# One copy for two pairs' attention output, and the first batch's tokens scaled with the batch they ride with

## The chip, the cores and the metric

The kernel runs on one core of one Trainium2 chip. The metric is device time in microseconds for one execution. The five engines are named as in the profile: PE (matrix multiply; PEld is its weight load), DVE (vector), ACT (scalar), POOL (GpSimd) and SP, which here only issues DMAs.

## The reference

With q and k of shape (8 batches, 12 heads, 448 tokens, 64) and v alike, the reference computes attention with a sigmoid in place of a softmax, joins the heads to 768 columns, and passes the result through a gated layer:

```python
scores = scale * np.matmul(q, k.transpose(0, 1, 3, 2)) - np.log(S)
attn = 1.0 / (1.0 + np.exp(-scores))
x = np.matmul(attn, v)                                   # heads joined: (8, 448, 768)
...
for k in range(K):                                       # K = 5
    gate_pre += conv_w[k][None, None, :] * xp[:, k:k + S, :]   # xp: x with 4 zero tokens ahead
gate = 1.0 / (1.0 + np.exp(-gate_pre))
val = x @ w_val
return (gate * val @ w_out)
```

All inputs and outputs are fp32.

## The kernel before, in words

**Work units.** A *pair* is two heads of one batch; there are 48 (six per batch), numbered i. Two pairs make a *two*, numbered j (24, three per batch). The columns of x that a pair yields are 128 of the 768, so a pair's x lies in SBUF as 128 partitions by 448 tokens.

**Attention.** For each pair, `scores` (L486 to L500) multiplies three blocks of 128 keys by the queries into a PSUM tile of two banks, one per head; the last 64 keys of both pairs of a two go through `scores_rest` (L502 to L513) into one such tile. `attention` (L515 to L532) applies the sigmoid on ACT. `attend` (L556 to L596) multiplies by the values: one PSUM tile `px` of two banks takes the x of both pairs of a two, bank p for pair p. It is written by five pieces of PE work that follow each other: the rest's (L578), then for p = 0 and p = 1 the key blocks 0 and 1, and the key block 2 (L586). All of these tiles come from one ring, `ps_a`, of three tiles, in the order rest, px, three for the even pair, three for the odd pair.

**Two precisions.** fp32 operands are multiplied in one of two ways. In the sets `WHOLE` (of twos, for attention times values) and `WHOLE_SCORES` (of pairs, for scores) the operands stay fp32. Otherwise they are split into a high and a low part and three cheaper products are summed: for `attend` in fp16, with values scaled by a power of two found by `v_scale` (L534 to L553) from the largest value (L564, spread over partitions by the matmul L574, read by DVE at L541); for scores by a copy and a subtraction (`split_qk`). A whole two needs one ACT operation for each score tile (L519) where a split one needs two on ACT (L519, L359) and one on DVE (L530).

**After attention.** `after` (L600 to L650) runs for each pair: it copies bank p of px to the tile x (L353 or L359 on ACT, L355 on DVE), finds the largest value on DVE (L619), and for batches 1 to 7 computes the gate: a copy of four tokens between segments (L641), the first tap (L359), four more taps on DVE (L647), a sigmoid (L650). Batch 0 has no products of its own: its 448 tokens are cut into seven runs of 64, and run f - 1 rides as 64 more columns with batch f, so that every product has 512 columns. So x of batch 0 goes to HBM (`first_x`) and a run of it is loaded with each later x tile (L634).

**Scaled products.** `x_scale` (L655) finds a batch's scale, `x_split` (L681) makes the high and low fp16 parts xs (L359 on ACT, L694 on DVE). In this version batch 0 has its own scale (`first_scale`), is split by itself, goes to HBM (`first_xs`) and comes back by run as the last 64 columns of xs. `product` (L702) multiplies 128 output columns: 18 matmuls of 512 columns (L716). For `val` DVE multiplies by the gate (L726), and the result g is split again; for `out` the result y is scaled in two operations, 448 columns with the batch's scale and 64 with batch 0's (L359 or L361), and stored by two DMAs.

**What sets the order.** Nothing is ordered by hand. Every operation is recorded with its possible engines, a cost, a priority (`tau` of its pair plus an entry of the table `AT`) and the buffers that it reads and writes; `Plan.issue` simulates the engines and so fixes the order in which each engine's instructions are emitted. The instructions then run in that order on each engine, and wait on semaphores that the tile layer derives from the tiles which each instruction touches. `Buf.part()` tells the plan that a part of a buffer may be used apart from the rest: in `attend`, `s["px"]` holds px and a part of it, so the plan takes the two banks as separate.

Of the kernel before, what the change touches and what calls it, by code (L numbers as in the profile page):

```python
# [10 lines left out]
F32 = mybir.dt.float32  # L11
# [13 lines left out]
KT = 5  # L25
P = 128
# [12 lines left out]
WHOLE = {*range(8)}  # L39
WHOLE_SCORES = {*range(15), 18}  # L40
# [33 lines left out]
    first=8.83, step=12.31, val=-38.5, val_step=7.32, out=-6, out_step=18.88, w_max=-5.5, w_split=-21.5,  # L74
    load_qk_first=-114, load_qk=93, load_v=-82, split_hi=38.5, split_lo=-9, rest_first=32, rest=138.5,
    a_first=-120, a=-70, attend=36, v_max=-106.5, v_exp=-11.5, v_split=-127, x=-60, x_max=-103,
    x_scale=-274, x_hi=-25, x_lo=-170, x_step=6.37, tap=81, scores=72, a_rest=38, a_rest_first=-111.5,
    tap_step=3.36, gate=-67.5, product=26, y=-45, g_hi=11, g_lo=-52.5, o=0.5, w_load=-41.5,
# [169 lines left out]
def attention_then_gate(  # L248
# [48 lines left out]
    x_ring = ring(sb, 9, [P, SEGS, HALO + SL], F32, "x")  # L297

    xs_ring = ring(sb, 8, [P, 2, T], F16, "xs")
# [31 lines left out]
    first_x = [scratch([P, HALO + S], F32, f"first_x{c}") for c in range(NC)]  # L331
    first_xs = [scratch([P, 2, S], F16, f"first_xs{c}") for c in range(NC)]
    first_scale = fixed([P, NC], F32, "first_scale")
# [153 lines left out]
    def scores(i, c):  # L487
# [11 lines left out]
        cost = (0.77 if i in WHOLE_SCORES else 0.61) + (0.1 if c == 0 else 0)  # L499
        return op({"P": cost}, tau(i) + AT["scores"], emit, sources(i), [b])  # L500

    def scores_rest(j):  # L502


        b = two[j]["ps"] = ps_a.new()
        x = [st[2 * j + n]["qk"] for n in range(2)]

        def emit(e):
            for n, to in enumerate(halves):
                for h, rows in enumerate(halves):  # L510
                    mm(b()[to, h, :S], x[n]()[rows, CW:], x[n]()[rows, :S], start=True, stop=True)  # L511

        return op({"P": 0.95}, tau(2 * j) + AT["rest_first" if 2 * j < AHEAD else "rest"], emit, x, [b])  # L513
# [20 lines left out]
    def v_scale(j):  # L534
# [3 lines left out]
        x, e, px = s["v"], v_exp.new(), two[j - 1]["px"][0]  # L538
        s["e"] = e
        col = lambda n: e()[:, n : n + 1]  # L540
        op({"V": 0.08}, tau(2 * j) + AT["v_exp"], lambda _: nc.vector.tensor_scalar(  # L541
            col(0), px()[:, 0, S : S + 1].bitcast(I32), 0x7F800000, None, op0=ALU.bitwise_and), [px], [e], port="")
# [13 lines left out]
    def attend(j):  # L556
# [3 lines left out]
        px, single, m = ps_a.new(), j in WHOLE, None  # L560
        s["px"] = px, px.part()
        if j + 1 < TWOS and j + 1 not in WHOLE:
            m, x = vm.new(), two[j + 1]["v"]
            op({"V": 0.98}, t + AT["v_max"], lambda e: nc.vector.tensor_reduce(  # L564
                m(), x(), axis=AX.X, op=ALU.max, apply_absolute_value=True), [x], [m], port="")
# [23 lines left out]
        last = first = op({"P": 0.87 if single else 0.75}, t, rest, [s["a"], *values] + ([ones, m] if m else []), s["px"])  # L589
        for p in range(2):  # L590
            for cs in ((0, 1), (2,)):
                last.then = op(
                    {"P": (0.82 if single else 0.64) * len(cs)}, t, lambda e, p=p, cs=cs: chunks(p, cs),
                    [*(st[2 * j + p]["a", c] for c in cs), *values], [s["px"][p]])
                last = last.then
# [4 lines left out]
    def after(i):  # L600

        s, t = st[i], tau(i - i % 2 + 2)
        p, f, c = i % 2, i // NP, i % NP
        px, whole = two[i // 2]["px"][p], i // 2 in WHOLE
        got = lambda: two[i // 2]["px"][0]()[:, p, :S]
        if c == 0:
            xm[f] = x_max.new()

        def out_of_ps(to, x):
            if whole:  # L610
                op({"A": 0.45, "V": 0.53}, t + AT["x"], lambda e: copy(e, to(), got()), [], [x, px], port="")
            else:
                v = two[i // 2]["e"]
                op({"A": 0.55}, t + AT["x"], lambda e: scaled(
                    e, to(), got(), v()[:, 3:4].bitcast(F32)), [v], [x, px], port="")

        def largest(to, x):
            b = xm[f]
# [3 lines left out]
        if f == 0:  # L622
            x = s["x"] = x_ring.new(lambda: sb.tile([P, HALO + S], F32, name="x_first", tag="x", bufs=x_ring.n))
            to = lambda: x()[:, HALO:].rearrange("p (s n) -> p s n", n=SL)
            s["own"], s["tokens"] = x, to
            op({"G": 0.1}, t - 8, lambda e: nc.gpsimd.memset(x()[:, :HALO], 0.0), [], [x], port="")
            out_of_ps(to, x)
            op({"S": 0.45}, t + 2, lambda e: nc.sync.dma_start(first_x[c](), x()), [x], [first_x[c]], P * 1800)
            largest(to, x)
            return  # L630
        x, g = s["x"], s["g"] = x_ring.new(), gate_ring.new()
        own, edge = x.part(), x.part()
        n = (f - 1) * SL
        op({"S": 0.45}, t - 8, lambda e: nc.sync.dma_start(  # L634
            x()[:, SEGS - 1, :], first_x[c]()[:, n : n + HALO + SL]), [first_x[c]], [x], P * 544)
        op({"G": 0.1}, t - 8, lambda e: nc.gpsimd.memset(x()[:, 0, :HALO], 0.0), [], [edge], port="")
        to = lambda: x()[:, : SEGS - 1, HALO:]
        s["own"], s["tokens"] = own, to
        out_of_ps(to, own)
        largest(to, own)  # L640
        op({"V": 0.1}, t + AT["tap"] - 0.5, lambda e: nc.vector.tensor_copy(  # L641
            x()[:, 1 : SEGS - 1, :HALO], x()[:, : SEGS - 2, SL:]), [own], [edge])
        by = lambda tile: tile.rearrange("p (s n) -> p s n", s=SEGS)
        w = lambda j: cw()[:, c, KT - 1 - j : KT - j]
        op({"A": 0.63, "V": 0.43}, t + AT["tap"], lambda e: scaled(e, by(g()), x()[:, :, HALO:], w(0)), [x, own, cw], [g])
        for j in range(1, KT):
            op({"V": 0.67}, t + AT["tap"] + AT["tap_step"] * j, lambda e, j=j: nc.vector.scalar_tensor_tensor(  # L647
                by(g()), x()[:, :, HALO - j : HALO + SL - j], w(j), by(g()), op0=ALU.mult, op1=ALU.add),
               [x, own, edge, cw], [g])
        op({"A": 0.55}, t + AT["gate"], lambda e: nc.scalar.activation(g(), g(), AF.Sigmoid), [], [g])  # L650
# [4 lines left out]
    def x_scale(b):  # L655
# [3 lines left out]
        for c in range(NP):  # L659
            st[b * NP + c]["xe"] = e  # L660
# [10 lines left out]
    def x_unscale(b):  # L671
        t = tau((b + 1) * NP) + AT["x_scale"] + 10
        e = st[b * NP]["xe"]
        to = outer[b] = o_scale.new() if b else first_scale
# [5 lines left out]
    def x_split(i):  # L680
        s, f, c = st[i], i // NP, i % NP  # L681
        t = tau((f + 1) * NP) + AT["x_step"] * c
        tokens, own, e = s["tokens"], s["own"], s["xe"]
        xs = s["xs"] = xs_ring.new()
        if f:
            n = (f - 1) * SL
            op({"S": 0.45}, t - 8, lambda _: nc.sync.dma_start(
                xs()[:, :, S:], first_xs[c]()[:, :, n : n + SL]), [first_xs[c]], [xs], P * 512)
        high, low = (xs.part() if f else xs), xs.part()
        s["xs_in"] = [xs, high, low]  # L690
        part = lambda n: xs()[:, n, :S].rearrange("p (s n) -> p s n", n=SL)
        sc = lambda: e()[:, 1:2].bitcast(F32)
        op({"A": 0.56, "V": 0.59}, t + AT["x_hi"], lambda eng: scaled(eng, part(0), tokens(), sc()), [own, e], [high])
        op({"V": 0.6}, t + AT["x_lo"], lambda _: nc.vector.scalar_tensor_tensor(  # L694
            part(1), tokens(), sc(), part(0), op0=ALU.mult, op1=ALU.subtract), [own, e, high], [low])
        if f == 0:
            op({"S": 0.45}, t + 2, lambda _: nc.sync.dma_start(first_xs[c](), xs()[:, :, :S]), [xs, low], [first_xs[c]], P * 1800)
# [4 lines left out]
    def product(n, b, m):  # L702
# [184 lines left out]
```

## Time and profile before

| | |
|---|---|
| three timed runs, median (lowest to highest) | 611.48 us (611.26 to 613.67) |
| the profiled execution | 611.03 us, of which the trace's span is 609.3 us |
| mean granted TensorE clock | 0.999 |
| PE busy | 580.9 us |
| DVE, ACT, POOL busy | 491.4, 409.3, 89.9 us |

The span runs from the first to the last instruction of the trace; the 1.7 us beside it lie around it. Of the views used, the windows give each engine's busy time in a stretch, the waits say for whom an engine sat idle, the timeline lists instructions with the idle time ahead of them, the groups sum instructions by line and shape, and the chain follows the work that ended last from releaser to releaser.

### The profile page before, as it was taken

The page shows a single profiled execution, that of the slowest core. Times are in us where ns is not written, and L with a number is a line of the kernel's source. Part 1 is how long each engine was busy: PE and PEld are TensorE (multiplying, and loading weights), DVE is VectorE, ACT ScalarE, POOL GpSimd, SP SyncE. Part 2 cuts the span into 40 slices and gives each one's busy share as a digit, 9 for nine tenths or more (in the row PEclk, how much of TensorE's full clock was granted, in tenths as well). Part 3 has the DMA queues.
Part 4 walks back from the last instruction along what each step waited for, and adds up shares of the span by engine and source line. Part 5 has one row for each costly group of instructions (what it writes and reads, how often), then busy time and mean ns, then how long its engine had stood idle before and what let it go on. Part 6 is the DMA issues. An engine that isn't in the chain of part 4 may idle for free.

```text
span 609.3 us, 9673 instructions
## 1 busy us (share of the span) xinstructions
PE 580.9 (95%) x3562; PEld 275.5 (45%) x3562; DVE 491.4 (81%) x893; ACT 409.3 (67%) x577; POOL 89.9 (15%) x120
## 2 busy tenths in 40 slices
PE   8899989999999999999999999999999999999996
PEld 4233324344444545444454444544444454444442
DVE  1899999899999889898888988879897797853310
ACT  5579877576985678857688676787757887642111
POOL 0000003210222212121221311113121131000000
PEclk9999999999999999999999999999999999999999
DMA  8998632232340332303234031341213300011011
GB/s 337 365 292 266 193 116 95 66 79 65 97 115 27 100 98 67 109 30 100 61 105 110 30 95 44 120 112 36 67 38 126 115 23 1 9 52 55 0 36 69
DMA packets 44351, 59.74 MB, mean 98 GB/s; under 512 B 25872, under 2 KB 33552, under 8 KB 44304
## 3 DMA queue, kind: packets, MB, share of 16 engines
q1 hardware_dynamic: 44304, 59.13, 31.0%
q8 instruction: 28, 0.46, 0.3%
q14 instruction: 19, 0.16, 0.1%
HBM read 45.34 MB, written 13.77 MB: 97 GB/s over the span
## 4 chain that ended last, share of the span: by engine, by line
PE 88%; DVE 5%; ACT 5%; issue 1%; ACTq 0%; DVEq 0%
PE ps_m L716 52%; PE ps_a L496 14%; PE ps_a L586 14%; PE ps_a L511 3%; PE ps_a L578 3%; ACT x L359 2%; ACT a_single L519 1%; DVE gate L647 1%; DVE x_max L619 1%; ACT y L359 1%; DVE w_words L381 1%; PE ps_m L751 1%; ACT xs L359 0%; ACT x L353 0%; DVE w_words L404 0%
## 5 line engine op out<-in xcount | busy, mean ns | idle before, releaser
L716 PE MATMUL ps_m<-g,w_out_hi 128*128 128x512 f16 x504 | 150.1, 379 | 1.4 <-DVE y L361 0.8
L716 PE MATMUL ps_m<-xs,w_val_hi 128*128 128x512 f16 x504 | 150.1, 379 | 0.8 <-DVE y L361 0.4
L364 POOL TENSOR_TENSOR qk_lo<-qk_src,qk_hi 128x448 fp32r<-128x448 f32 x64 | 81.8, 1291 | 305.2 <-DVE qk_hi L355 207.3
L647 DVE SCALAR_TENSOR_TENSOR gate<-x,cw,gate 128x512 f32<-128x512 f32 x168 | 125.5, 768 | 0.4 <-ACT gate L359 0.2
L519 ACT ACTIVATE ps_a<-ps_a 128x896 f32<-128x896 f32 x112 | 98.7, 902 | 17.5 <-PE ps_a L496 16.2
L530 DVE SCALAR_TENSOR_TENSOR a<-ps_a,a 128x896 f16<-128x896 f32 x96 | 101.4, 1084 | 9.2 <-ACT a L359 8.0
L716 PE MATMUL ps_m<-g,w_out_lo 128*128 128x512 f16 x252 | 95.5, 379 | 0.0
L716 PE MATMUL ps_m<-xs,w_val_lo 128*128 128x512 f16 x252 | 95.5, 379 | 0.0
L359 ACT ACTIVATE a<-ps_a 128x896 f16<-128x896 f32 x96 | 84.6, 920 | 0.4
L716 PEld LDWEIGHTS <-w_out_hi 128*128 128x128 f16 x504 | 48.0, 98 | 62.1 <-issue 5.9
L716 PEld LDWEIGHTS <-w_val_hi 128*128 128x128 f16 x504 | 47.8, 98 | 62.4 <-issue 7.5
L586 PE MATMUL ps_a<-a,v_hi 128*64 128x448 f16 x384 | 53.1, 355 | 11.6 <-ACT x L359 11.6
L519 ACT ACTIVATE a_single<-ps_a 128x896 f32<-128x896 f32 x56 | 47.3, 923 | 5.4 <-PE ps_a L496 3.6
L359 ACT ACTIVATE y<-ps_m,o_scale 128x448 f32<-128x448 f32 x35 | 21.5, 629 | 42.4 <-PE ps_m L716 35.3
L353 ACT CAST g<-y 128x512 f16<-128x512 f32 x24 | 14.8, 618 | 50.8 <-DVE y L726 50.5
L726 DVE SCALAR_TENSOR_TENSOR y<-ps_m,y_scale,gate 128x512 f32<-128x512 f32 x42 | 29.6, 742 | 20.3 <-PE ps_m L716 20.3
L586 PE MATMUL ps_a<-a_single,v_src 128*64 128x448 f32 x192 | 39.6, 547 | 6.2 <-ACT x L353 2.9
L650 ACT ACTIVATE gate<-gate 128x512 f32<-128x512 f32 x42 | 26.1, 626 | 26.5 <-DVE gate L647 26.3
L619 DVE TENSOR_REDUCE x_max<-x 128x1 f32<-128x448 f32 x42 | 25.8, 614 | 21.1 <-ACT x L359 19.0
L496 PE MATMUL ps_a<-qk_single 64*128 64x448 f32 x192 | 40.1, 554 | 0.4 <-ACT a_single L519 0.4
L359 ACT ACTIVATE x<-ps_a,v_exp 128x448 f32<-128x448 f32 x32 | 20.3, 634 | 29.5 <-PE ps_a L586 25.4
L496 PE MATMUL ps_a<-qk_hi 64*128 64x448 f32 x192 | 38.5, 397 | 0.0
(110 smaller groups left out, 728.0 us busy)
## 6 DMA issues: line engine op xcount, KB each, us to landing
qk_src<-qk SPq DMA_DIRECT2D x32, 448.0 KB, 4.0
v_src<-vs SPq DMA_DIRECT2D x24, 448.0 KB, 3.4
out_t<-y SPq DMA_DIRECT2D x42, 224.0 KB, 2.0
qk_single<-qk SPq DMA_DIRECT2D x16, 448.0 KB, 5.5
w_words<-w_val SPq DMA_DIRECT2D x6, 768.0 KB, 9.4
w_words<-w_out SPq DMA_DIRECT2D x6, 768.0 KB, 4.9
x<-first_x SPq DMA_DIRECT2D x42, 34.0 KB, 2.0
first_x<-x_first SPq DMA_DIRECT2D x6, 226.0 KB, 5.7
```

The lines of the kernel that those rows point to most:

```text
L359: nc.scalar.activation(to, x, AF.Copy, scale=by)
L364: engines[eng].tensor_tensor(to, x, y, op=ALU.subtract)
L496: mm(b()[:, h, :S], k()[rows, at : at + P], q()[rows, :S], start=(n == 0), stop=(n == len(terms(i)) - 1))
L511: mm(b()[to, h, :S], x[n]()[rows, CW:], x[n]()[rows, :S], start=True, stop=True)
L519: nc.scalar.activation(to, b()[:, :, :S], AF.Sigmoid, bias=-math.log(S), scale=1.0 / math.sqrt(D))
L530: op({"V": 1.0}, t + 0.5, lambda e: nc.vector.scalar_tensor_tensor(part(1), p(), A_SCALE, part(0), op0=ALU.mult, op1=ALU.subtract), [b], [ ...
L586: mm(px()[to, p, :S], v()[:, o : o + D], x(st[2 * j + p]["a", c])[:, h, at : at + S], start=False, stop=(c == 2 and n == len(parts) - 1), ...
L619: op({"V": 0.52}, t + AT["x_max"], lambda e: nc.vector.tensor_reduce(b()[:, c : c + 1], to(), axis=AX.XY, op=ALU.max, apply_absolute_value ...
L647: op({"V": 0.67}, t + AT["tap"] + AT["tap_step"] * j, lambda e, j=j: nc.vector.scalar_tensor_tensor(by(g()), x()[:, :, HALO - j : HALO + S ...
L650: op({"A": 0.55}, t + AT["gate"], lambda e: nc.scalar.activation(g(), g(), AF.Sigmoid), [], [g])
L716: mm(po(), w()[:, c, :], x()[:, k, :], start=(c == 0 and j == 0), stop=(c == NC - 1 and j == 2))
L726: op({"V": 0.6}, t + AT["y"], lambda e: nc.vector.scalar_tensor_tensor(y(), po(), y_scale()[:, m : m + 1], gate(), op0=ALU.mult, op1=ALU.m ...
```

## The change

1. `attend` writes px as one buffer, and `after` runs once for each two: one operation copies both banks (2 x 448 columns) into one tile x of two pairs, which has one load of batch 0's run, one search for the largest value and one edge copy. The ring of x has 5 such tiles (was 9 single ones), that of xs 4 (was 8).
2. Batch 0 has no scale, no split and no `first_xs`: the largest value of a batch f is taken over its own tokens and the run that rides with it, one `x_split` operation takes 2 x 512 columns, and y of an `out` product is scaled by one operation of 512 columns. Batch 0's tokens are thus rounded with another scale than before.
3. The search for the largest value of v and its matmul move from `attend`, where they used a column of px of the two before, to `scores_rest`, where they use a column of the rest's bank; DVE reads it there (`v_exp`).
4. `WHOLE` is now twos 0 to 8 and 21 (was 0 to 7), `WHOLE_SCORES` pairs 0 to 14, 17, 24, 39, 42, 43 (was 0 to 14 and 18).
5. The priorities in `AT` and some costs have other numbers; two lines of the table stand here for all.

```diff
-WHOLE = {*range(8)}
-WHOLE_SCORES = {*range(15), 18}
+WHOLE = {*range(9), 21}
+WHOLE_SCORES = {*range(15), 17, 24, 39, 42, 43}
...
-    first=8.83, step=12.31, val=-38.5, val_step=7.32, out=-6, out_step=18.88, w_max=-5.5, w_split=-21.5,
+    first=8.2, step=11.51, val=-64.5, val_step=38.05, out=-42, out_step=46.57, w_max=-113, w_split=-46.5,
...
-    x_ring = ring(sb, 9, [P, SEGS, HALO + SL], F32, "x")
-    xs_ring = ring(sb, 8, [P, 2, T], F16, "xs")
+    x_ring = ring(sb, 5, [P, 2, SEGS, HALO + SL], F32, "x")
+    xs_ring = ring(sb, 4, [P, 2, 2 * T], F16, "xs")
...
     def scores_rest(j):
+        if j not in WHOLE:
+            m, v = vm.new(), s["v"]
+            op({"V": 0.98}, t + AT["v_max"], lambda e: nc.vector.tensor_reduce(
+                m(), v(), axis=AX.X, op=ALU.max, apply_absolute_value=True), [v], [m], port="")
         def emit(e):
+            if m:
+                mm(b()[:, 0, S : S + 1], ones(), m(), start=True, stop=True)
...
+        if m:
+            e = s["e"] = v_exp.new()
+            op({"V": 0.08}, t + AT["v_exp"], lambda _: nc.vector.tensor_scalar(
+                e()[:, :1], b()[:, 0, S : S + 1].bitcast(I32), 0x7F800000, None, op0=ALU.bitwise_and), [], [b, e], port="")
...
     def attend(j):
-        s["px"] = px, px.part()
+        s["px"] = px
...
-    def after(i):
+    def after(j):
-        got = lambda: two[i // 2]["px"][0]()[:, p, :S]
-                op({"A": 0.45, "V": 0.53}, t + AT["x"], lambda e: copy(e, to(), got()), [], [x, px], port="")
+            got = lambda: px()[:, :, :S].rearrange("p t (s n) -> p t s n", n=SL)
+                op({"A": 0.82, "V": 1.0}, t + AT["x"], lambda e: copy(e, to(), got()), [], [x, px], port="")
-                op({"A": 0.55}, t + AT["x"], lambda e: scaled(
+                op({"A": 0.95}, t + AT["x"], lambda e: scaled(
                     e, to(), got(), v()[:, 3:4].bitcast(F32)), [v], [x, px], port="")
...
-            op({"V": 0.52}, t + AT["x_max"], lambda e: nc.vector.tensor_reduce(
-                b()[:, c : c + 1], to(), axis=AX.XY, op=ALU.max, apply_absolute_value=True), [x], [b], port="")
+        op({"V": 1.1}, t + AT["x_max"], lambda e: nc.vector.tensor_reduce(
+            b()[:, 2 * c : 2 * c + 2], x()[:, :, :, HALO:], axis=AX.XY, op=ALU.max, apply_absolute_value=True),
+           [x, own], [b], port="")
...
     def x_split
-            op({"S": 0.45}, t - 8, lambda _: nc.sync.dma_start(
-                xs()[:, :, S:], first_xs[c]()[:, :, n : n + SL]), [first_xs[c]], [xs], P * 512)
-        op({"A": 0.56, "V": 0.59}, t + AT["x_hi"], lambda eng: scaled(eng, part(0), tokens(), sc()), [own, e], [high])
+        op({"A": 1.16, "V": 1.19}, t + AT["x_hi"], lambda eng: scaled(eng, part(0), tokens(), sc()), [x, own, e], [high])
...
     def product
-            op({"A": 0.54, "V": 0.6}, t + AT["o"], lambda e: scaled(e, y()[:, :S], po()[:, :S], col(b)), [outer[b]], [y, po], port="")
-            op({"A": 0.21, "V": 0.2}, t + AT["o"], lambda e: scaled(e, y()[:, S:], po()[:, S:], col(0)), [po, outer[0]], [low], port="")
+            op({"A": 0.61, "V": 0.66}, t + AT["o"], lambda e: scaled(
+                e, y(), po(), outer[b]()[:, m : m + 1]), [po, outer[b]], [y], port="")
```

**What the new order looks like.** On ACT, from the sigmoid of the rest's tile of two 12 (`ps_a_2267`) on, while PE multiplies two 11 by its values into `ps_a_2279`, there stood before:

```order
L519 ACTIVATE ps_a_2267<-ps_a_2267 128x2x448
L650 ACTIVATE gate_2052<-gate_2052 128x512
L359 ACTIVATE a_rest_2315<-ps_a_2267 128x2x448
L650 ACTIVATE gate_2146<-gate_2146 128x512
L359 ACTIVATE x_1685<-ps_a_2279,v_exp_2061 128x7x64
L359 ACTIVATE gate_2338<-x_1685,cw_68 128x512
L359 ACTIVATE x_1693<-ps_a_2279,v_exp_2061 128x7x64
L359 ACTIVATE gate_2369<-x_1693,cw_68 128x512
L359 ACTIVATE v_hi_2380<-v_src_1858,v_exp_2347 128x896
L519 ACTIVATE ps_a_2352<-ps_a_2352 128x2x448
```

At the same two now (`ps_a_1936` is the rest's tile, `ps_a_1948` is px, the three tiles behind are the next pair's scores), ACT has:

```order
L531 ACTIVATE ps_a_1936<-ps_a_1936 128x2x448
L359 ACTIVATE a_rest_1982<-ps_a_1936 128x2x448
L648 ACTIVATE gate_1894<-gate_1894 128x512
L359 ACTIVATE x_1658<-ps_a_1948,v_exp_1694 128x2x7x64
L531 ACTIVATE ps_a_2013<-ps_a_2013 128x2x448
L531 ACTIVATE ps_a_2021<-ps_a_2021 128x2x448
L359 ACTIVATE a_2038<-ps_a_2013 128x2x448
```

The two copies of px with a tap between them have become one, which stands ahead of the sigmoids of the next scores; the first taps and the splitting of v have moved elsewhere.

On DVE around the same place there stood before, from the second half of the rest's tile on:

```order
L530 SCALAR_TENSOR_TENSOR a_rest_2315<-ps_a_2267,a_rest_2315 128x2x448
L619 TENSOR_REDUCE x_max_1784<-x_1685 128x1
L541 TENSOR_SCALAR v_exp_2347<-ps_a_2279 128x1
L641 COPY x_1685<-x_1685 128x6x4
L543 TENSOR_SCALAR v_exp_2347<-v_exp_2347 128x1
L647 SCALAR_TENSOR_TENSOR gate_2338<-x_1685,cw_68,gate_2338 128x512
L545 TENSOR_SCALAR v_exp_2347<-v_exp_2347 128x1
```

And now, where the first two rows are the gating of the products that PE finished just ahead of the rest:

```order
L717 SCALAR_TENSOR_TENSOR y_1942<-ps_m_1878,y_scale_103,gate_1044 128x512
L717 SCALAR_TENSOR_TENSOR y_1944<-ps_m_1884,y_scale_103,gate_1085 128x512
L523 TENSOR_SCALAR v_exp_1961<-ps_a_1936 128x1
L645 SCALAR_TENSOR_TENSOR gate_1894<-x_1176,cw_68,gate_1894 128x512
L552 TENSOR_SCALAR v_exp_1961<-v_exp_1961 128x1
L364 TENSOR_TENSOR g_1946<-y_1942,g_1946 128x512
L554 TENSOR_SCALAR v_exp_1961<-v_exp_1961 128x1
L364 TENSOR_TENSOR g2_1964<-y_1944,g2_1964 128x512
L556 TENSOR_SCALAR v_exp_1961<-v_exp_1961 128x1
L645 SCALAR_TENSOR_TENSOR gate_1894<-x_1176,cw_68,gate_1894 128x512
L542 SCALAR_TENSOR_TENSOR a_rest_1982<-ps_a_1936,a_rest_1982 128x2x448
L361 TENSOR_SCALAR v_hi_2017<-v_src_1509,v_exp_1961 128x896
```

The read of v's largest value (`v_exp`, first row of it) has moved from px to the rest's tile and from behind the rest's work to ahead of it.

On PE the pieces of a two stand in the same order as before, but the first pair of products stands behind the eighth attention times values (it stood behind the seventh), so that about 20 products are left behind the last one where 16 were.

More of the change, by code (lines that the diff above doesn't have):

```diff
@@ L559, in attend @@
         s, t = two[j], tau(2 * j + 2) + AT["attend"]
-        px, single, m = ps_a.new(), j in WHOLE, None
-        s["px"] = px, px.part()
[L562 to L565, printed above, removed]
+        px, single = ps_a.new(), j in WHOLE
+        s["px"] = px
         values = [s["v"]] if single else [s["vh"], s["vl"]]
@@ L587, in chunks @@
                            start=False, stop=(c == 2 and n == len(parts) - 1), skip_group_check=True)
[L589 removed]
+        last = first = op({"P": 0.86 if single else 0.8}, t, rest, [s["a"], *values], [px])
         for p in range(2):
             for cs in ((0, 1), (2,)):
[L592 to L594 removed]
+                cost = (0.752 if single else 0.567) * len(cs) + (0.13 if p and cs == (2,) else 0)
+                last.then = op({"P": cost}, t, lambda e, p=p, cs=cs: chunks(p, cs),
+                               [*(st[2 * j + p]["a", c] for c in cs), *values], [px])
                 last = last.then
@@ L622, in after @@
[L622 to L630, printed above, removed]
@@ L646, in after @@
[L646 to L650, printed above, removed]
+            x()[:, :, SEGS - 1, :], first_x[c]()[:, :, n : n + HALO + SL]), [first_x[c]], [x], P * 1088)
@@ new lines, in after @@
+        by = lambda tile: tile.rearrange("p (s n) -> p s n", s=SEGS)
+        for p in range(2):
+            g = st[2 * j + p]["g"] = gate_ring.new()
+            w = lambda k, p=p: cw()[:, 2 * c + p, KT - 1 - k : KT - k]
+            at = t + AT["tap"] + AT["tap_pair"] * p
+            op({"A": 0.63, "V": 0.43}, at, lambda e, p=p, g=g, w=w: scaled(
+                e, by(g()), x()[:, p, :, HALO:], w(0)), [x, own, cw], [g])
+            for k in range(1, KT):
+                op({"V": 0.67}, at + AT["tap_step"] * k, lambda e, p=p, g=g, w=w, k=k: nc.vector.scalar_tensor_tensor(
+                    by(g()), x()[:, p, :, HALO - k : HALO + SL - k], w(k), by(g()), op0=ALU.mult, op1=ALU.add),
+                   [x, own, edge, cw], [g])
+            op({"A": 0.55}, t + AT["gate"] + AT["tap_pair"] * p, lambda e, g=g: nc.scalar.activation(
+                g(), g(), AF.Sigmoid), [], [g])
@@ L658, in x_scale @@
         m, d, e, po = xm[b], diagonal.new(), x_exp.new(), ps_m.new()
-        for c in range(NP):
-            st[b * NP + c]["xe"] = e
+        for c in range(3):
+            two[3 * b + c]["xe"] = e
         col = lambda n: e()[:, n : n + 1]
@@ L672, in x_unscale @@
         t = tau((b + 1) * NP) + AT["x_scale"] + 10
-        e = st[b * NP]["xe"]
-        to = outer[b] = o_scale.new() if b else first_scale
+        e = two[3 * b]["xe"]
+        to = outer[b] = o_scale.new()
         op({"V": 0.06}, t, lambda _: nc.vector.tensor_scalar(
@@ L821, in attention_then_gate @@
             continue
+        x_scale(b)
+        for c in range(3):
+            x_split(3 * b + c)
         if b > 1:
```

117 lines of the change are left out of this document (49 added, 68 removed).

## The prediction

> **What bounds the kernel now.** I read the engines' totals, then stretches of 26 us, then PE's own waits, then one repeat of the loop in order of time. The totals (busy us, share of the span, instructions), the granted clock by slices, and the chain's shares by engine:
>
> ```profile
> PE 580.9 (95%) x3562; PEld 275.5 (45%) x3562; DVE 491.4 (81%) x893; ACT 409.3 (67%) x577; POOL 89.9 (15%) x120
> ...
> PEclk9999999999999999999999999999999999999999
> ...
> PE 88%; DVE 5%; ACT 5%; issue 1%; ACTq 0%; DVEq 0%
> ```
>
> PE is the bound nearly everywhere, at the full clock. The span of 609.3 us less 580.9 leaves 28.4 us of idle PE. Two stretches of the loop, first column the stretch, then its length, then busy us of PE, PEld, DVE, ACT and POOL:
>
> ```profile
> 334.00:360.00 26.00, 25.27 (x167) 12.67 (x165) 23.23 (x41) 18.07 (x25) 5.32 (x4) 1.00 0.17 54
> ...
> 464.00:490.00 26.00, 25.27 (x167) 12.73 (x168) 22.64 (x47) 22.23 (x33) 4.58 (x7) 1.00 0.32 98
> ```
>
> PE idles the same 0.73 us in each, DVE is 87 to 89% busy, ACT 70 to 86%. Whom PE waits for (us in total, times, longest):
>
> ```profile
> PE ps_a L586 <- ACT x L359: 11.6, 16, 0.7
> PE ps_a L586 <- ACT x L353: 2.9, 4, 0.9
> PE ps_a L586 <- ACT x_first L353: 1.9, 3, 0.6
> PE ps_m L414 <- DVE out_inverse L418: 1.5, 1, 1.5
> PE ps_a L586 <- ACT gate L359: 1.4, 1, 1.4
> ```
>
> The four rows of L586 are 16 + 4 + 3 + 1 = 24 waits, one for each two, and 17.8 us in all: well over half of PE's idle time, all in the same line. The row of L414 I keep for the range. In the chain, the starts of two rests that follow each other give the length of one repeat, 351.88 - 325.93 = 25.95 us:
>
> ```profile
> 325.93 0.91 PE ps_a L511 x8
> ...
> 351.88 0.91 PE ps_a L511 x8
> ```
>  One of the waits in order of time (start, us, engine and line, idle time and releaser in brackets):
>
> ```profile
> 329.12 1.09 DVE L530 SCALAR_TENSOR_TENSOR a_rest<-ps_a,a_rest 128x896 f16<-128x896 f32 x1 [1.26 <-ACT a_rest L359]
> ...
> 330.24 0.36 PE L586 MATMUL ps_a<-a,v_lo 128*64 128x448 f16 x2
> ...
> 330.64 0.63 ACT L359 ACTIVATE x<-ps_a,v_exp 128x448 f32<-128x448 f32 x1 [1.55 <-PE ps_a L586]
> ...
> 331.33 0.57 PE L586 MATMUL ps_a<-a,v_hi 128*64 128x448 f16 x4 [0.73 <-ACT x L359]
> ...
> 332.02 0.47 PE L496 MATMUL ps_a<-qk_hi 64*128 64x448 f32 x2
> ...
> 332.31 0.64 ACT L359 ACTIVATE x<-ps_a,v_exp 128x448 f32<-128x448 f32 x1 [0.28 <-DVE v_exp L541]
> ...
> 333.34 0.36 PE L496 MATMUL ps_a<-qk_hi 64*128 64x448 f32 x2
> ```
>
> PE has just multiplied into bank 1 (pair p = 1, key blocks 0 and 1), ending at 330.60. ACT then copies bank 0, 330.64 to 331.27, and only at 331.33 does PE go on with key block 2 of bank 1. The copy reads bank 0, the matmuls write bank 1: no data passes between them. The copy stands between two writes of the same tile, and the semaphores follow the tile, not the bank, though the plan took the banks for separate buffers. So every two pays one copy in PE time.
>
> **The change part by part.**
>
> *The wait goes.* Now the only copy of px stands behind its last matmul, so nothing is left between the pieces of `attend`: - 17.8 us.
>
> *What is late next: the copy itself.* px must be empty when the third score tile behind it starts, since the ring has three tiles. In the rows above the first score matmul starts at 332.02 and the third tile (`333.34`) 1.32 us later, without a wait. The price of a copy of 2 x 448 columns comes from the same operation at two widths and from an ACT operation with a scale from SBUF at 896 (groups by line and shape; behind the bar busy us and mean ns; some rows serve further down):
>
> ```profile
> L647 DVE SCALAR_TENSOR_TENSOR gate<-x,cw,gate 128x512 f32<-128x512 f32 x168 | 125.5, 768 | 0.4 <-ACT gate L359 0.2
> ...
> L519 ACT ACTIVATE ps_a<-ps_a 128x896 f32<-128x896 f32 x112 | 98.7, 902 | 17.5 <-PE ps_a L496 16.2 <-PE ps_a L511 1.1
> ...
> L650 ACT ACTIVATE gate<-gate 128x512 f32<-128x512 f32 x42 | 26.1, 626 | 26.5 <-DVE gate L647 26.3
> ...
> L359 ACT ACTIVATE y<-ps_m,o_scale 128x448 f32<-128x448 f32 x35 | 21.5, 629 | 42.4 <-PE ps_m L716 35.3 <-issue 6.9
> ...
> L359 ACT ACTIVATE x<-ps_a,v_exp 128x448 f32<-128x448 f32 x32 | 20.3, 634 | 29.5 <-PE ps_a L586 25.4 <-DVE v_exp L541 4.0
> ...
> L530 DVE SCALAR_TENSOR_TENSOR a_rest<-ps_a,a_rest 128x896 f16<-128x896 f32 x16 | 17.5, 1091 | 15.7 <-ACT a_rest L359 15.6
> ...
> L359 ACT ACTIVATE a_rest<-ps_a 128x896 f16<-128x896 f32 x16 | 14.6, 913 | 0.5 <-ACT ps_a L519 0.2
> ...
> L359 ACT ACTIVATE v_hi<-v_src,v_exp 128x896 f16<-128x896 f32 x11 | 11.3, 1026 | 0.0
> ...
> L359 ACT ACTIVATE y<-ps_m,first_scale 128x64 f32<-128x64 f32 x17 | 5.1, 309 | 0.0
> ...
> L541 DVE TENSOR_SCALAR v_exp<-ps_a 128x1 int32<-128x1 int32 x16 | 2.5, 157 | 2.9 <-PE ps_a L586 2.9
> ...
> L666 PE MATMUL ps_m<-diagonal,ones 128*128 128x128 bf16 x8 | 1.8, 225 | 0.4 <-DVE y L361 0.4
> ```
>
> From 64 to 448 columns y grows by 320 ns, 0.83 ns a column; 634 + 448 x 0.83 = 1.01 us, close to the 1.03 of v_hi. With 0.04 us from PE's end to ACT's start (330.60 to 330.64) and 0.06 back (331.27 to 331.33) the tile is free 1.11 us behind the last matmul, 0.2 us before PE asks. For that ACT must be idle when PE ends. In the trace it is: it sat idle 1.55 us ahead of the first copy. In the new order a sigmoid of a gate (0.63 us) stands there instead, and the rest's sigmoid now waits for DVE's short read of v's maximum. I count 0.05 us for each of the 24: + 1.2 us, with 0 and 0.25 each (6 us) as ends, the upper being half a gate sigmoid late less the 0.2 of slack, rounded up.
>
> A rule of the Trainium skill speaks against this step: Perfetto Trace Analysis, Optimizing Scalar/DVE Operations, says that where ScalarE is not saturated but causes bubbles elsewhere, breaking up its instructions may let work finish sooner. ACT here is 67% busy and does cause PE's bubbles, so by the rule the two short copies should stay, and the sum would keep the 17.8 us in place of the 1.2 (615.1 us). The trace differs in one point: the early copy is what PE waits for, so breaking up made the bubble. What the rule gets right is the first rival below.
>
> *More matmul time.* Pieces of the chain (start, us, line, instructions) of a whole two, of a split one, and of one pair's scores either way:
>
> ```profile
> 24.24 0.75 PE ps_a L578 x8
> 24.99 3.93 PE ps_a L586 x20
> ...
> 54.23 0.97 PE ps_a L586 x4
> ...
> 326.95 0.69 PE ps_a L578 x12
> 327.64 2.98 PE ps_a L586 x30
> ...
> 331.33 0.76 PE ps_a L586 x6
> ...
> 69.90 2.46 PE ps_a L496 x12
> ...
> 332.09 2.02 PE ps_a L496 x18
> ```
>
> Whole: 0.75 + 3.93 + 0.97 = 5.65 us; split: 0.69 + 2.98 + 0.76 = 4.43. Two more whole twos (8 and 21) cost 2 x 1.22 = 2.4 us. Whole scores cost 2.46 - 2.02 = 0.44 more; the set has 20 pairs where it had 16, + 1.8 us. Nothing hides this, since PE is the bound: + 4.2 us.
>
> *Less work beside PE.* A whole two drops seven ACT operations and seven DVE operations of about 1 us, and its v needs no split. One largest value, one low part and one scaled y take the place of two operations each; batch 0's six splits and its DMAs go. All of it lies on engines that PE does not wait for in the windows: 0 now. If DVE were the bound it would be worth some microseconds, so this also covers the shorter repeat: with 0.73 us less, 23.2 us of DVE work would still fit the 25.2 left, before any of it is dropped. Merging as such costs at most 0.2 us per operation where a consumer waits for the first half, and those consumers (taps, split) have a period or more.
>
> *Small terms on PE.* Batch 0's scale needed a matmul (0.22 us); it goes: - 0.2 us. v's maximum is the same matmul at another place: 0. Products start one two later and 20 instead of 16 stand alone at the end. There PE waits for y at each pair of products; after scaling in two operations and after one:
>
> ```profile
> 572.26 0.59 PE L716 MATMUL ps_m<-xs,w_val_hi 128*128 128x512 f16 x2 [0.20 <-DVE y L726]
> ...
> 588.79 0.59 PE L716 MATMUL ps_m<-g,w_out_hi 128*128 128x512 f16 x2 [0.44 <-DVE y L361]
> ```
>
> Two more pairs at 0.20 add 0.4; some three pairs of `out` that fall from 0.44 to about 0.20, since y is one operation now, save 0.7. I take 0, with 0.5 us either way. The last y is one operation of about 629 + 64 x 0.83 = 0.68 us for one of 0.63 and one of 0.31: 0 again.
>
> *The sum.* 609.3 - 17.8 + 1.2 + 4.2 - 0.2 = 596.7 us of span. The profiled execution took 611.03 us, 1.7 more than its span, so 598.4; it lies 0.45 us below the median of the runs (611.48). Rounded between the two: 598.5 us.
>
> **The rivals.**
>
> *The copy comes late (no change).* This is the skill's rule as a mechanism here: bank 0 is no longer emptied early, so all of px hangs on one ACT operation behind the last matmul. If ACT starts the gate's sigmoid (0.63 us) just as PE ends, px is free at 0.63 + 1.11 = 1.74 us against 1.32 asked, a wait of 0.42. In every two that is 24 x 0.42 = 10.1 us less the 1.2 counted: 607.4. From 0.3 to 0.55 us a two it is 604.5 to 610.5. Chance 0.08. For it: ACT and DVE queues run in order. Against: whole scores ask only 1.64 us behind (eight of twelve matmuls of 2.46 us), which gives every early two 0.5 us of slack, and ACT had 1.55 us idle at this place.
>
> *DVE holds the rest (slower).* The rest's sigmoid now waits for DVE's read of v's maximum, which stands behind two gating operations. From the rest's last matmul to the free rest tile it takes 0.16 (read) + 0.90 (sigmoid) + 0.91 (its high part) + 1.09 (DVE's low part) and about 0.3 for four hand-overs, 3.4 us; the second score tile asks for it 0.69 + 2.98 + 0.76 + 0.66 = 5.1 us behind. So DVE may be 1.7 us late before PE pays, and 13.0 / 14 = 0.9 us beyond that before the gain is gone in the 14 twos that have the read (24 less 10 whole ones): the point is 2.6 us late, over three taps of 0.77. At 3.5 us it costs 14 x 1.8 = 25 us: 623.5 us. Against: at 87 to 89% busy DVE reached its parts without making PE wait once in these windows. Chance 0.05.
>
> *The wait does not go.* If the last piece of `attend` really waited for something else that ended with the copy (its own tile of attention, say), 17.8 stays: 611.0 + 4.2 - 0.2 = 615.0. Against: the bracket names the copy 24 times of 24 or the ACT operation behind it, and PE starts 0.06 us after it ends. Chance 0.02.
>
> **How the numbers follow.** The forecast has 0.85: about 598.5 us, on its own 595.7 (no new wait, and the 1.5 us of the L414 row gone) to 604 (0.25 us at each copy and 0.5 at the end). The late copy takes the range up to 606. So 595.5 to 606. A measurement of this kernel can tell about 0.5% from no change, 3.1 us, so faster means below 608.4. Faster: 0.85 and a little from the late copy, 0.86; same: the rest of that, 0.07; slower: 0.05 + 0.02 = 0.07.
>
> **What would show it.** Right: PE's waits for x at the line of `attend` fall from 24 to none; the repeat of the loop shrinks from 25.95 to about 25.2 us; x takes about 1.0 us on ACT; PE busy rises by about 4 us. Wrong: a new row of PE at the score line (L496) waiting for ACT x or DVE a_rest, of more than 0.25 us each; or the old gap still ahead of the last piece. If PE busy itself came out more than 6 us higher, the price of the whole products would be wrong.

## The result, and the profile after

| | before | after |
|---|---|---|
| median of 4 runs (lowest to highest) | 611.44 us (611.26 to 613.67) | 592.10 us (591.62 to 592.37) |
| profiled execution, its span | 611.03, 609.3 us | 592.33, 590.5 us |
| PE busy | 580.9 us | 578.1 us |

The ratio is 0.9675, with a 95% interval of 0.9651 to 0.9698: faster, by 19.3 us where 12.9 were forecast, and below the range. The direction and the main mechanism were right. The step that failed is the first term of the sum, mis-sized: the wait was entered at 17.8 us, and 22.6 went with it. Two terms put at nothing failed beside it; the section on the prediction has them. One run of 2900 us, of the twelve of one experiment, is left out of its median.

The totals of after, and the granted clock by slices:

```profile
PE 578.1 (98%) x3503; PEld 273.4 (46%) x3503; DVE 463.4 (78%) x766; ACT 366.9 (62%) x478; POOL 70.5 (12%) x88
...
PEclk9999999999999999999999999999999999999999
```

PE busy was to rise by 4 us and fell by 2.8. The span less PE busy leaves 12.4 us idle (28.4 before). The same two stretches as in the prediction, now:

```profile
334.00:360.00 26.00, 25.74 (x170) 12.98 (x169) 23.60 (x39) 17.82 (x24) 4.04 (x5) 1.00 0.17 54
464.00:490.00 26.00, 26.00 (x173) 13.16 (x170) 22.15 (x37) 17.90 (x22) 2.24 (x3) 1.00 0.14 45
```

PE now idles 0.26 us in one and not at all in the other. PE's waits (us in total, times, longest):

```profile
PE ps_a L496 <- DMA qk_single<-qk: 1.4, 1, 1.4
PE ps_m L707 <- ACT y L359: 1.1, 3, 0.8
...
PE ps_a L496 <- ACT x L353: 0.7, 2, 0.4
...
PE ps_a L496 <- DVE a_rest L542: 0.5, 2, 0.3
```

All 24 waits at the line of `attend` (L586 before, L589 now) are gone. The copy of px delays the scores twice (0.7 us in all), both in the first 92 us. It costs what was worked out, 1.01 us (groups):

```profile
L359 ACT ACTIVATE x<-ps_a,v_exp 128x896 f32<-128x896 f32 x14 | 14.1, 1007 | 11.1 <-PE ps_a L589 11.1
```

Why did 17.8 us of waits make more room than 17.8 us? The end of one `attend` in time on PE, of before and then of after:

```profile
356.20 0.35 PE L586 MATMUL ps_a<-a,v_lo 128*64 128x448 f16 x2
357.28 0.57 PE L586 MATMUL ps_a<-a,v_hi 128*64 128x448 f16 x4 [0.73 <-ACT x L359]
```

```profile
352.69 0.35 PE L589 MATMUL ps_a<-a,v_lo 128*64 128x448 f16 x2
352.88 0.55 PE L589 MATMUL ps_a<-a,v_hi 128*64 128x448 f16 x4
353.26 0.35 PE L589 MATMUL ps_a<-a,v_lo 128*64 128x448 f16 x2
353.54 0.47 PE L496 MATMUL ps_a<-qk_hi 64*128 64x448 f32 x2
```

The two rows that follow each other start 1.08 us apart with the wait and 0.19 without: 0.89 us, where the bracket says 0.73. In these rows of an unbroken stream a matmul starts before the one ahead has ended (352.88 against 352.69 + 0.35); with the wait it starts 0.73 behind that end, and the bracket counts only this part. So PE's gains are better read from start to start, and so are all pieces below. Likewise at the matmul of v's largest value, before and after:

```profile
351.50 0.38 PE L716 MATMUL ps_m<-xs,w_val_lo 128*128 128x512 f16 x1
351.81 0.98 PE L511 MATMUL ps_a<-qk_src 64*64 64x448 f32 x8
352.72 0.18 PE L574 MATMUL ps_a<-vm,ones 128*128 128x1 bf16 x1
352.83 0.57 PE L578 MATMUL ps_a<-a_rest,v_hi 64*64 64x448 f16 x8
```

```profile
348.22 0.38 PE L707 MATMUL ps_m<-xs,w_val_lo 128*128 128x512 f16 x1
348.44 0.17 PE L515 MATMUL ps_a<-vm,ones 128*128 128x1 bf16 x1
348.54 0.98 PE L518 MATMUL ps_a<-qk_src 64*64 64x448 f32 x8
349.34 0.56 PE L581 MATMUL ps_a<-a_rest,v_hi 64*64 64x448 f16 x8
```

From the first row to the last it takes 1.33 us with the column behind the rest's eight, 1.12 ahead of them. No idle time is shown in either.

PE's time by kind of piece (summed from the start of each piece to the start of the next, us; the warm-up matmuls of the first 3 us are left out):

| | scores | rest and v's column | attend | products | scales of weights and x | sum of these |
|---|---|---|---|---|---|---|
| before | 104.1 | 24.1 | 135.0 | 333.4 | 4.3 | 600.9 |
| after | 110.9 | 21.6 | 114.4 | 331.8 | 3.0 | 581.7 |

So the 19.2 us are -20.6 in `attend`, -2.5 at the rest, -1.6 in products, -1.3 at scales, and +6.8 in scores.

### The profile page after: what moved, and what is told of

Same layout as the page of the kernel before. It is cut to its first block, busy times and chain, and to the rows that moved or that the text cites. A ratio compares the mean times of both kernels' runs of the same rounds, so it can differ in the third digit from the quotient of the medians.

```text
span 590.5 us, 9085 instructions
## 1 busy us (share of the span) xinstructions
PE 578.1 (98%) x3503; PEld 273.4 (46%) x3503; DVE 463.4 (78%) x766; ACT 366.9 (62%) x478; POOL 70.5 (12%) x88
## 5 line engine op out<-in xcount | busy, mean ns | idle before, releaser
L364 POOL TENSOR_TENSOR qk_lo<-qk_src,qk_hi 128x448 fp32r<-128x448 f32 (+1 forms) x56 | 64.7, 1171 | 300.5 <-DVE qk_hi L355 111.3
L542 DVE SCALAR_TENSOR_TENSOR a<-ps_a,a 128x896 f16<-128x896 f32 x84 | 89.0, 1082 | 4.8 <-ACT a L359 4.5
L531 ACT ACTIVATE ps_a<-ps_a 128x896 f32<-128x896 f32 x98 | 86.7, 906 | 8.6 <-DVE v_exp L523 7.8
L359 ACT ACTIVATE a<-ps_a 128x896 f16<-128x896 f32 x84 | 74.5, 924 | 0.3
L531 ACT ACTIVATE a_single<-ps_a 128x896 f32<-128x896 f32 x70 | 60.0, 922 | 7.2 <-PE ps_a L496 4.7
L359 ACT ACTIVATE y<-ps_m,o_scale 128x512 f32<-128x512 f32 x38 | 25.5, 686 | 60.6 <-PE ps_m L707 53.8
L496 PE MATMUL ps_a<-qk_single 64*128 64x448 f32 x240 | 51.1, 555 | 2.2 <-DMA qk_single<-qk 1.4
L353 ACT CAST g<-y 128x512 f16<-128x512 f32 x33 | 20.5, 620 | 52.6 <-DVE y L717 52.2
L589 PE MATMUL ps_a<-a_single,v_src 128*64 128x448 f32 x240 | 47.3, 543 | 0.0
L589 PE MATMUL ps_a<-a,v_hi 128*64 128x448 f16 x336 | 46.1, 354 | 0.0
L707 PEld LDWEIGHTS <-w_val_lo 128*128 128x128 f16 x252 | 24.7, 98 | 29.7
L707 PEld LDWEIGHTS <-w_out_lo 128*128 128x128 f16 x252 | 24.6, 98 | 29.8
L359 ACT ACTIVATE gate<-x,cw 128x512 f32<-128x512 f32 x32 | 23.1, 735 | 20.1 <-DVE y L717 20.1
```

Source lines behind the costliest of these rows:

```text
L353: nc.scalar.copy(to, x)
L359: nc.scalar.activation(to, x, AF.Copy, scale=by)
L364: engines[eng].tensor_tensor(to, x, y, op=ALU.subtract)
L496: mm(b()[:, h, :S], k()[rows, at : at + P], q()[rows, :S], start=(n == 0), stop=(n == len(terms(i)) - 1))
L531: nc.scalar.activation(to, b()[:, :, :S], AF.Sigmoid, bias=-math.log(S), scale=1.0 / math.sqrt(D))
L542: op({"V": 1.0}, t + 0.5, lambda e: nc.vector.scalar_tensor_tensor(part(1), p(), A_SCALE, part(0), op0=ALU.mult, op1=ALU.subtract), [b], [ ...
```

## Experiments

Twelve kernels ran, each beside runs of before on the same chip (611.56 to 611.82 us). Before's medians differ by up to 0.4 us between these chips and that of the result, so a difference of half a microsecond between two kernels is read from their traces. The first four were planned anew; the later ones keep the planned order of the kernel named, but for the operations that the edit moves.

**Both copies behind, in before.** The plan is told that px has no parts:

```diff
-        s["px"] = px, px.part()
+        s["px"] = px, px
```

> The kernel before, with one edit: the plan takes px as one buffer, so both of its copies (still two operations of 448 columns) stand behind the last matmul of the two. Nothing else of the change. Theory A (a wait of PE costs its idle gap and, beside it, the overlap of matmuls that is lost when PE starts again, about 0.9 us a two from start to start, where the profile showed 0.74 idle): 24 x 0.9 = 21.6 us less, given back by 1 to 3 us where the two copies (0.04 + 2 x 0.63 + 0.06 = 1.37 us) come just too late for the third score tile (1.32): 590.5 to 593. The pieces of attention times values of a split two should take 3.53 us from start to start where they took 4.44. Rival B (a wait costs its idle gap alone, 17.8 us): 594.5 to 597. Rival C (the merged operation and the lighter queues bring the gain, not the place of the copies): above 603.

Measured: 669.05 us, ratio 1.0923 (1.0892 to 1.0953). `attend` lost its waits (3.53 us a split two, 4.44 before), but the new plan lays products out so that PE waits elsewhere:

```profile
PE ps_m L716 <- ACT y L359: 17.9, 8, 3.1
PE ps_a L496 <- DVE a L530: 17.2, 9, 3.8
```

This measures another order, not the wait. The mean granted clock was 0.964 besides (below).

**Two copies in after.** `out_of_ps` records one operation for each bank, both behind the last matmul.

> The changed kernel, with px copied by two operations of 448 columns, both behind the last matmul. Theory A: the gain comes from where the copies stand; two copies free px at 1.37 us in place of 1.1, against 1.32 asked by split scores: 0.05 to 0.1 us in each of 13 split twos, and none at whole scores (1.64 asked): 592 to 594. Rival C (one operation is what brings it): most of it lost, above 597.

Measured: 613.59 us (1.0017, 1.0001 to 1.0033), again by another order (7.3 us of PE waiting at L496 for DVE's a).

**The old sets in after.** `WHOLE` and `WHOLE_SCORES` as before (so other operands are split):

> The changed kernel, with the sets of whole twos and pairs as before. PE has less to multiply: two twos at 1.31 us and four pairs at 0.44, 4.4 us. Theory F (PE is the bound everywhere, the added whole ones only cost): 587 to 588.5. Rival G (where DVE is 95% busy, 100 to 204 us, the tenth and the extra pairs spared it more than they cost PE): 592 or more, with new waits of PE for DVE in that stretch.

Measured: 615.18 us (1.0054, 1.0041 to 1.0068); PE waits 8.3 us for y and 5.8 for a. The mean granted clock was 0.989. The order is another one here too, so what the sets alone are worth stays open.

**v's column behind the rest, in after.** The matmul of one column is emitted behind the rest's eight:

```diff
-            if m:
-                mm(b()[:, 0, S : S + 1], ones(), m(), start=True, stop=True)
             for n, to in enumerate(halves):
                 ...
+            if m:
+                mm(b()[:, 0, S : S + 1], ones(), m(), start=True, stop=True)
```

> The changed kernel, with the one-column matmul of the largest v behind the eight matmuls of the rest, not ahead of them; same tile, same number. Theory D (its place on PE is worth about 0.2 us a split two: the rest takes 0.91 to 0.92 us where it stands behind and 0.80 where it stands ahead, and the products ahead of it 7.87 and 7.78): 14 x 0.2 = 2.8 us more, 594.9. Rival E (the place is worth nothing, the shorter rest and products come from something else, such as fewer DMAs): 592.1, the rest still at 0.80.

Measured: 594.33 us (0.9714, 0.9701 to 0.9727), 2.2 more than after (the edit lies within one piece of PE work, and the plan came out the same): the place of 14 one-column matmuls is worth 0.16 us each.

**The order of before, both copies behind.** The planned list is kept; the two copies of px, and what hangs on them, move behind the last matmul of `attend`:

```diff
+    todo = plan.issue()
+    for j in range(TWOS):
+        a, b, c = copies[2 * j], copies[2 * j + 1], last_of[j]
+        ...
+        todo[n:n] = [a, b, *held]
```

> The kernel before, with its planned order kept for every engine, except that the copy of px's first bank and what hangs on it are moved behind the last matmul of the two, both copies next to each other. PE's order is that of before, word for word. Theory A (a wait of PE costs its idle gap and the restart of the matmul pipeline, 0.85 to 0.91 us a two from start to start): 24 waits less, 21.3 us, given back by up to 2 us where the second copy comes 0.05 us late for the third score tile: 590 to 593. Rival B (the idle gap alone, 17.8 us): 593.7 to 596. Rival C (the single operation and the lighter queues are what brings the gain): above 600.

Measured: 610.16 us (0.9974, 0.9964 to 0.9984). The total is that of rival C. `attend` fell by 21.1 us (its last pieces by 22.1; 0.85 to 0.92 for 22 of the 24 waits), so the price of the wait held; but scores rose by 11.0, products by 4.0, scales of weights and x by 5.1. Some of the waits behind that:

```profile
PE ps_a L496 <- ACT a_single L519: 3.7, 4, 2.0
...
PE ps_m L414 <- DVE out_inverse L418: 1.8, 1, 1.8
...
PE ps_m L716 <- DVE x_exp L667: 1.3, 2, 0.7
```

About half of the loss (9.7 us by start to start) lies ahead of 95 us, where ACT and DVE convert weights (DVE is busy 78 of the 80 us from 20 to 100 in before): PE met sigmoids and scales that were not ready, the first two rows. The rest lies behind 95 us: 5.4 in scores, 4.0 in products (some wait for the scale of x, the third row) and 1.9 in the scales of x. After one of the early waits the granted clock fell; PE's row, and three stretches of 5 us with the clock in the third column from the end:

```profile
22.41 3.93 PE L496 MATMUL ps_a<-qk_single 64*128 64x448 f32 x12 [1.97 <-ACT a_single L519]
```

```profile
20.00:25.00 5.00, 3.04 (x13) 1.34 (x13) 4.44 (x10) 4.22 (x6) 0.00 (x0) 0.85 1.03 401
25.00:30.00 5.00, 5.00 (x31) 1.47 (x29) 4.08 (x12) 3.45 (x4) 0.00 (x0) 0.81 0.48 140
30.00:35.00 5.00, 5.00 (x30) 1.93 (x24) 3.82 (x7) 1.94 (x3) 0.00 (x0) 1.00 0.84 289
```

That is 5 x 0.15 + 5 x 0.19 = 1.7 us of full clock lost, and the same again at 90 us. Not every such wait has this sequel (see the end). Later, every second piece of scores of a split two takes 2.33 us where it took 2.02. One of them:

```profile
331.97 0.47 PE L496 MATMUL ps_a<-qk_hi 64*128 64x448 f32 x2
332.08 1.16 ACT L359 ACTIVATE x<-ps_a,v_exp 128x448 f32<-128x448 f32 x2 [2.13 <-PE ps_a L586]
...
333.28 0.15 DVE L541 TENSOR_SCALAR v_exp<-ps_a 128x1 int32<-128x1 int32 x1
...
333.49 0.19 PEld L496 LDWEIGHTS ps_a<-qk_hi 64*128 64x128 f32 x2 [0.40 <-DVE v_exp L541]
```

The weight load of the third score tile waits for DVE's read of v's largest value, which lies in px and comes behind the copies. The change's third part takes this value out of px. Two runs test that.

**The same, with the read first.** DVE's read stands ahead of the search for the largest x, the matmul stays in px.

> As the kernel with both copies behind in the order of before (610.16 us), with one operation moved on DVE: the read of v's largest value stands ahead of the search for the largest x; the matmul keeps its place in px. Theory P (px is held by that read): the second scores piece falls from 2.33 to at most 2.07 us: 605.9, within 605 to 607. Theory Q (the copies hold px): 609.5 to 610.5.

Measured: 611.84 us (0.9995, 0.9981 to 1.0008); the piece stayed at 2.31 to 2.34 in most twos. The total is neither theory's; the mean granted clock of the twelve runs lay between 0.990 and 0.999, so the piece is the better measure.

```profile
253.01 0.47 PE L496 MATMUL ps_a<-qk_hi 64*128 64x448 f32 x2
...
253.12 0.16 DVE L543 TENSOR_SCALAR v_exp<-ps_a 128x1 int32<-128x1 int32 x1 [1.00 <-PE ps_a L588]
...
253.32 1.16 ACT L359 ACTIVATE x<-ps_a,v_exp 128x448 f32<-128x448 f32 x2 [2.32 <-DVE v_exp L543]
```

Theory P fell: the copies now start behind the read, 0.31 us after the score matmul instead of 0.11. In either order the two readers of px ran one behind the other, as in a row that the prediction shows of before: the second copy waits 0.28 us for v_exp L541. Why they do was not tried.

**The same, with v's column and its read in the rest's tile,** as the change has it:

> The version before in its own order, both copies of px behind its last matmul (610.16 us as such), and now also the change's third part: the largest value of v goes through a matmul ahead of the rest's eight, into the rest's tile, and DVE reads it there. Theory P (with one copy behind, px is held by DVE's read of v's largest value, which stands behind the search for the largest x): the second scores piece of the 14 split twos falls from 2.33 to 2.02 us, 14 x 0.31 = 4.3 less, and the one-column matmul's place saves 14 x 0.2 = 2.8: 603.0, within 602 to 604.5. Theory Q (the piece waits for the copies themselves): it stays at 2.2 or more, only the 2.8 go: 607.4. Theory R (the read, now ahead in DVE's queue, waits for PE and holds back what is queued behind it): 609 or more.

Measured: 605.82 us (0.9898, 0.9885 to 0.9911), 4.3 less than with the value in px; PE's last matmul ended 5.9 us earlier in the profiled executions (7.1 expected). The piece fell to 2.13 in most twos, not to 2.02: 0.2 was the read, and 0.11 the two copies (1.16 us) where one takes 1.01; the kernel below with two operations in after's order has the same 2.13.

**Two operations in place of one, in after's order.** The same copy, bank by bank, one directly behind the other:

> The changed kernel with its planned order kept; the one copy of px becomes two operations of 448 columns, one behind the other at the same place. Theory A: px is free 1.37 us behind the last matmul in place of 1.11, asked at 1.32 by split scores and 1.64 by whole ones: 0 to 0.1 us more in each of 13 split twos, 592.3 to 593.6. Rival C: above 596.

Measured: 592.64 us (0.9686, 0.9672 to 0.9700). The 0.5 us more than after are no clearer than the chips; in the trace eight pieces of scores behind split twos take 2.12 to 2.15 us where after has 2.02 to 2.04. So merging as such is worth 0.5 to 0.8 us.

**Bank 0 copied early, in after's order.** The copy of bank 0 is emitted ahead of the last piece, as in before:

> The changed kernel with its planned order kept; bank 0 of px is copied ahead of the last piece of attention times values (as before the change), bank 1 where the one copy stood. This puts the wait back and nothing else. Theory A: attention times values of a split two 4.44 us from start to start again, of a whole one 5.51: 24 waits, 21.5 us, less up to 2 us that the shorter last copy wins at the scores: 612 to 613.6. Rival B (idle gap alone): 609 to 610.

Measured: 612.25 us (1.0009, 1.0000 to 1.0017), 20.2 more than after, by three rows:

```profile
PE ps_a L593 <- ACT x L359: 11.3, 14, 1.1
PE ps_a L593 <- ACT x L353: 6.3, 7, 1.7
PE ps_a L593 <- ACT x_first L353: 2.2, 3, 1.0
```

This is the change's core undone alone: with the wait back, nothing of the gain is left. The 20.2 us are a net price: by start to start `attend` takes 24.7 us more than in after and scores 3.9 less. The idle rows of these 24 waits sum to 19.8 us, 2.0 more than in before.

**Early work put back, in after's order.** Twelve DVE operations and six on ACT, about as batch 0 had of its own; no output uses them.

```diff
+        nc.vector.tensor_reduce(more_max()[:, p : p + 1], x, axis=AX.XY, op=ALU.max, apply_absolute_value=True)
+        nc.vector.scalar_tensor_tensor(by(more_lo()), x, cw()[:, 0, :1], x, op0=ALU.mult, op1=ALU.subtract)
```

> After in its own order, with work put back that changes no output: in batch 1 each of the three searches for the largest x is followed on DVE by two further searches and two low parts of 448 columns (12 operations, about 7.8 us), and each of the six first taps on ACT by one high part (6 operations, about 3.9 us), as batch 0 had of its own before. Theory L (the lighter queues of the first 100 us are part of the gain): at least 595, since DVE has 39 of 40 us busy there. Theory N (the dropped work lay beside PE, worth 0, as predicted): 591.8 to 593.

Measured: 599.72 us (0.9807, 0.9794 to 0.9819), 7.6 more than after (6.2 in the profiled executions, nearly all of it ahead of 100 us):

```profile
PE ps_a L496 <- ACT x L353: 3.5, 2, 2.3
PE ps_a L518 <- ACT a_single L531: 2.8, 3, 2.1
```

One of these, of 2.11 us, is again followed by a stretch with the clock at 0.66. So work of this kind is not free there. It stands at 55 to 95 us, where before had batch 0's at 16 to 56 us, so 7.6 us is the price of a like amount and not of that very work.

**The second pair's load ahead of the first v load, in after's order** (PE's 1.4 us for qk_single in after):

> The changed kernel with its planned order kept, except that the load of the first v is issued behind that of the second pair's q and k, not ahead of it. In the changed kernel PE's first scores wait 1.42 us for that load, which they did not before. Theory H (the span's start is PE's too, so a wait there is paid in full): 1.4 to 1.6 us less, 590.6. Rival I (the wait moves to the first attention times values, which needs v and the sigmoids): 592.1.

Measured: 591.54 us (0.9667, 0.9652 to 0.9681). The wait was not in the profile, nor was it in the last three kernels above, which have after's order with the loads untouched; the first 24 scores took 5.92 us, where in kernels whose loads were not touched they took 4.71, 4.71, 5.71 and 5.89 (the four in before's order) and 5.73 to 6.40 (after's). That piece varies by itself, so 0.6 us can't be put down to the load.

**That, and two weight steps behind the copy of px on ACT** (the two waits for x L353):

> The version with the second pair's load ahead of the first v load (591.54 us), and at two places (about 78 and 90 us) the copy of px stands ahead of the weight conversion step that ACT had ahead of it. Theory S (that step makes the copy late, and PE pays): the scores piece at 79 us falls by 0.1, that at 88 us from 5.69 to 4.5 us: 590.2, within 589.8 to 590.7. Rival: the weights then come late in turn and PE waits for them at the matmul that spreads their largest value: 591.3 or more.

Measured: 592.45 us (0.9684, 0.9672 to 0.9697). Both waits for x went; PE then waited 2.0 us for out_max at L414, and a piece of 30 score matmuls grew from 5.69 to 6.47 us. The rival held: the weights were late instead. No version was found that beats after by more than the runs differ.

## Why the prediction was right in kind and short in size

- **"The wait goes: - 17.8."** Right in kind: put back alone, it costs 20.2 us net. This is the step that failed, by its size, the largest error of the sum: 22.6 us in place of 17.8. The steps by start to start: -20.3 for the pieces behind the rest's, and two of them are now whole, at 1.13 more each: -22.6; in the kernel of before with its own sets -22.1. The idle rows of 17.8 us left out about 0.2 us of lost overlap for each of 24.
- **"More matmul time: + 4.2."** Held: whole less split is 1.31 a two and 0.44 a pair, 2 x 1.31 + 4 x 0.44 = 4.4.
- **"What is late next: + 1.2."** The arithmetic of the copy held (1.01 us), and PE met the copy itself twice. But scores rose 6.8 where 1.8 + 1.2 were in the sum: 1.8 whole pairs, 1.7 in the first piece, which varies by itself, and 3.3 in new waits, over half of them ahead of 95 us.
- **The repeat.** From the start of `attend` of two 9 to that of two 22 it is 337.7 us before and 326.8 after: 25.98 and 25.14 us a repeat, where 25.95 and 25.2 were given.
- **"v's maximum is the same matmul at another place: 0."** Wrong by 2.2 us, and for a second reason too: in px the value would have held the tile 0.2 us longer, in each split two, once the copy stands behind. A place on PE has a price, and so has the tile that a value lives in.
- **"Less work beside PE: 0 now."** This failed too, though the sum hides it. The windows at 334 and 464 us show DVE with room; from 20 to 100 us it has almost none, and the prediction shows no row of DVE or ACT there. A like amount of early work put back costs 7.6 us. With before's work and order only 1.7 of the 22 us stay (of what went, some 3.4 is the lower clock after two waits, and 14 x 0.31 = 4.3 the longer second pieces of scores). How the rest divides between lighter queues, other sets and the newly fitted table is open: that run keeps all three as before, and the three kernels whose plan came out different were 20 us or more slower than the kernel that they edit.
- **Batch 0's scale and products.** - 0.2 and 0 forecast, - 1.3 and - 1.6 measured; of the scales, 0.9 is the wait at L414 that the prediction kept for its range (1.5 us before, 0.6 now), and of the products, 14 x 0.09 = 1.3 is the column again (7.87 to 7.78 us for the two products ahead of it).
- **The rivals.** The late copy and "DVE holds the rest" both happened, for 0.7 us of PE's idle rows (two waits) and 0.5 (two); by start to start the second delayed three pieces of scores, by 1.4 us. The prediction weighed a rule of the Trainium skill (Perfetto Trace Analysis, Optimizing Scalar/DVE Operations): breaking up instructions may let work finish sooner. It went the other way here: broken up behind the last matmul the copy costs 0.5 to 0.8 us more, broken up around it 20.2.
- **How the errors add up.** The wait's - 4.8, - 2.5 at the rest and - 2.7 at scales and products lie on one side, + 3.8 in scores on the other. So the forecast came as near as it did partly by luck.

## What to carry to other kernels

Price a wait of a pipelined engine by start to start, against a place where the same two instructions follow without it: the idle row is a lower bound. Before a removed wait is credited, look at the stretch where the other engines are fullest, not at the steady loop, and list every reader of the buffer whose release becomes late. And an order that was fitted to one program can't judge a one-line edit: keep the order, or measure the order.

## What the runs showed of the hardware

A wait of PE of about 2 us can cost nearly twice its length. After some waits of 1.72 to 2.25 us the granted clock fell, each time by the same 1.7 us in sum:

```profile
545.14 0.22 PE L668 MATMUL ps_m<-diagonal,ones 128*128 128x128 bf16 x1 [2.17 <-DVE y L361]
```

```profile
540.00:545.00 5.00, 2.97 (x14) 1.27 (x13) 3.78 (x8) 2.01 (x4) 0.00 (x0) 1.00 0.00 0
545.00:550.00 5.00, 4.66 (x14) 1.76 (x14) 4.55 (x12) 2.85 (x6) 0.00 (x0) 0.67 0.31 107
550.00:555.00 5.00, 5.00 (x24) 2.28 (x23) 1.42 (x4) 0.44 (x1) 0.00 (x0) 0.99 0.00 0
```

These are of the kernel with the read first: 5 x 0.33 + 5 x 0.01 = 1.7. In the same execution 1.96 us of waiting at 21 us had no such effect, nor had 2.30 us in the kernel with early work put back, nor before's 1.47 us, so the length alone does not decide. The traces' clock records show more. Low stretches come in seven of the fourteen executions ahead of PE's last matmul: all are at half clock, 3.41 or 6.83 us long, and in each execution they start on a grid of 3.41 us. Of the grid's windows at full clock, all 19 with over 1.74 us of idle PE were followed by a low one, none with under 1.65 us was, and of six between them three were. The wait above leaves 2.10 us of idle PE in one window; the equally long wait at 546 us of the kernel with both copies behind in before's order is cut by the grid, which leaves 1.60 in its first window. So it matters where the wait falls. The kernel at 669 us lost 0.036 x 669 = 24 us in this way. The Trainium skill, TensorE: Matmul & The Clock Gate, HAM oscillation, how this bites in real kernels, gives "no PE-idle gaps >~3.4µs" as the rule. The traces here show the clock halved after shorter waits, so the measurement decides: 1.72 us can be enough.
